# Convolution of the later batches in fp16 halves: three half-precision products in place of one fp32 product

## The chip, the cores and the metric

The kernel runs on one core of one Trainium2 chip. The metric is device time in microseconds, from three runs of a kernel. The engines are PE (TensorE, the matrix engine), DVE (VectorE), ACT (ScalarE), POOL (GpSimd) and SP (SyncE, which here only starts transfers). ACT and POOL start transfers too. Each engine works through its own list of instructions in order and waits on semaphores for the others.

## The reference

The input `x` is 8 batches of 4224 tokens of 192 numbers in fp32. The work for each batch is a short causal convolution over tokens (7 taps, one set of taps for each of 8 heads of 24 columns), then the real part of a two-dimensional Fourier transform added to its input, a normalisation, and a two-layer perceptron with a residual:

```
w = softmax(weight, axis=-1)                     # (8 heads, 7 taps)
x_pad = concat([zeros(B, 6, D), x], axis=1)
conv[b, s, h, g] = sum_k w[h, k] * x_pad[b, s + k, h, g]
mixed = real(fft(fft(conv, axis=1), axis=2))
u = conv + mixed
un = (u - mean(u)) / sqrt(var(u) + 1e-6)
out = u + maximum(un @ w_ch1, 0) @ w_ch2
```

## The kernel before

**The convolution.** `conv_unit` (L400) works on a chunk of six windows of 120 tokens. A chunk lies in SBUF as `xt`, 128 rows (120 tokens and the ones ahead of them) by six windows by 192 columns, in fp32. For a head, one fp32 product of the banded matrix `band[:, h, :120]` (128 rows by 120 columns) with the 144 columns of that head (6 windows of 24) gives the head's output in the PSUM tile `pc`; L419 is that product. Three heads share one `pc`, so a chunk has three parts (3, 3 and 2 heads), and ACT carries each part from PSUM to `xa` (L428). From there a transfer writes it to `sc` in device memory, from which the Fourier stage reads it in another order. There are six chunks in a batch. The last batch computes seven heads this way, and the eighth on DVE (`conv_segments`).

**Batches overlap.** The main loop goes through steps; there are nine for a batch, numbered by `it` (the last is a short one). A step runs the perceptron for 512 tokens: six `ph` groups of five products (L792), each carried out of PSUM by ACT as `hh` (L796) and by DVE as `hlo` (L797, the rounding error of `hh`), and the `po` products of the step before (L811, L814, L817), whose sums DVE adds to `u` (L823). Between these units the loop spreads the front work of later batches: the convolution (one chunk in a step, over six steps), the loads of `xs` and their split into fp16 halves `XH` (ACT, L530) and `XL` (DVE, L538), and the first Fourier stage `pa` (L555, out of PSUM as `yh` and `yl`). The second stage `pb` (L581, carried out as `V`), the third `pq` (L678, added to `u` by DVE), and the normalisation come further on: DVE takes the statistics `mv`, POOL makes `v`, `y`, `un` and `hl` of them (L723 to L749), and a transposing transfer on SP (L763) turns `hl` into `kt`, which the `ph` products read. Batches 0 and 1 go through a start of their own, ahead of the loop or in its first steps.

**What sets the order.** The builder places each instruction in its engine's list when it builds the program, by its own estimate of when the inputs are there; the code only says what comes ahead of what. So code that is added in one place can move instructions elsewhere. The PSUM tiles `pc`, `pa`, `pb`, `pq` and `pn` share four buffers (tag `f`), `ph` has two, and `po` two.

**Norms.** `squares` (L357) squares a chunk on ACT and leaves the sum of each row in `nrm`. At the end of a batch's convolution `pow2_of_norm` (L211) adds these over all rows with a product by a matrix of ones (L218, `pn`), and takes the power of two `s_x` from it, by which `XH` and `XL` are scaled.

Of the kernel before, what the change touches and what calls it, by code (L numbers as in the profile page):

```python
# [126 lines left out]
def kernel(  # L127
# [30 lines left out]


# [199 lines left out]
    def squares(bt, x, behind=None):  # L359
        if bt.nsq == 0:  # L360
            bt.nrm = sb.tile([128, NCH + 1], F32, tag="nrmx", name=f"nrm_{bt.b}")
        n = x.shape[1] if len(x.shape) == 2 else x.shape[1] * x.shape[2]
        sq = sb.tile(
            [128, 1152], mybir.dt.bfloat16, tag="sq", name=f"sq_{bt.b}_{bt.nsq}", bufs=1
        )[:, :n]
        if len(x.shape) == 3:
            sq = sq.rearrange("p (w d) -> p w d", w=x.shape[1])
# [30 lines left out]

    def conv_unit(bt, ch, part, xa_slot=("xa", 2), slot=("f", 4), home=None):

        b = bt.b
# [15 lines left out]
        with after(staged.get("pe") if b == 1 else None):  # L417
          for h in range(h0, h0 + n):
            nc.tensor.matmul(  # L419
                pc[:WR, h - h0], band[:, h, :WR], xt[:, :, h * GRP : (h + 1) * GRP],  # L420
                start=True, stop=True,
            )
# [686 lines left out]
```

## Time and profile before

| | |
|---|---|
| time, median of 3 runs | 1238.72 us (1238.15 to 1240.5) |
| the profiled execution's own time | 1238.39 us |
| its span, from the first to the last instruction | 1236.6 us |
| mean granted clock of PE | 0.983 |
| PE busy | 1171.4 us (95%) |
| DVE, POOL, ACT busy | 818.3 us (66%), 768.3 us (62%), 595.6 us (48%) |
| products of the convolution | 756 records, two for each fp32 product |

Busy time of PE is the time in which at least one product is under way. Products overlap in the pipeline, so the duration of one (286 ns for a record of the fp32 convolution) is longer than its share of PE's time; what counts there is the distance from one start to the next. Idle time is put down to what ended it.

### The profile page before, as it was taken

What the parts mean: (1) busy time and instruction counts of PE and PEld (TensorE: products, weight loads), DVE (VectorE), ACT (ScalarE), POOL (GpSimd) and SP (SyncE); (2) the same over time, 40 slices, a digit from 0 to 9 for tenths busy, and PEclk for the clock granted to TensorE, in tenths of its full rate; (3) what the DMA queues carried; (4) which work ended last, traced back from release to release, by engine and by line L of the source; (5) the groups of instructions that cost most, each with busy time, mean ns of one, the idle gap of its engine ahead of it and who ended that gap; (6) DMA issues with size and microseconds to landing.
All of it is one profiled execution on the core that took longest, in us unless ns stands there. A gap on an engine that the chain in (4) does not pass through costs nothing.

```text
span 1236.6 us, 30122 instructions
## 1 busy us (share of the span) xinstructions
PE 1171.4 (95%) x12236; PEld 928.6 (75%) x12236; DVE 818.3 (66%) x1871; ACT 595.6 (48%) x983; POOL 768.3 (62%) x1103
## 2 busy tenths in 40 slices
PE   5289869999999999999999999999999999999998
PEld 4178657787878777787787878787687877787776
DVE  6777655687656975478656876468965687567543
ACT  5675545365544555446543565445454455333222
POOL 0207676479637785468854796467963688667840
PEclk9599989999999999999999999999999999999999
DMA  8964985566455756377645675557754643323321
GB/s 297 271 189 115 240 125 114 128 173 185 93 123 149 186 140 140 87 181 188 144 96 138 157 194 100 123 144 185 150 99 100 164 99 90 83 63 81 81 56 42
DMA packets 238506, 170.47 MB, mean 138 GB/s; under 512 B 119512, under 2 KB 222112, under 8 KB 238368
## 3 DMA queue, kind: packets, MB, share of 16 engines
q1 hardware_dynamic: 184888, 109.95, 38.9%
q10 hardware_dynamic: 46952, 45.24, 13.4%
q0 software_dynamic: 6528, 13.38, 4.4%
q8 instruction: 95, 1.56, 0.5%
q14 instruction: 43, 0.35, 0.1%
HBM read 83.82 MB, written 58.55 MB: 115 GB/s over the span
## 4 chain that ended last, share of the span: by engine, by line
PE 85%; DVE 7%; DMA 4%; ACT 1%; issue 1%; POOL 1%; SPq 1%; DVEq 0%; ACTq 0%; POOLq 0%
PE ph L792 32%; PE po L811 10%; PE po L817 10%; PE po L814 10%; PE pa L555 6%; PE pb L581 6%; PE pq L678 6%; PE pc L419 6%; DVE XL L538 1%; DMA xs<-sc 1%; DVE yl L564 1%; DVE hlo L797 1%; DVE u L696 1%; DMA xs_yh<-sc 1%; ACT XH L530 1%
## 5 line engine op out<-in xcount | busy, mean ns | idle before, releaser
L792 PE MATMUL ph<-kt,W 128*128 128x512 f16 (+1 forms) x2160 | 494.9, 362 | 8.6 <-DVE hlo L797 7.0
L797 DVE SCALAR_TENSOR_TENSOR hlo<-ph,hh 128x512 f16<-128x512 f32 (+1 forms) x400 | 271.3, 679 | 279.0 <-ACT hh L796 271.1
L796 ACT ACTIVATE hh<-ph 128x512 f16<-128x512 f32 (+1 forms) x400 | 237.0, 593 | 432.1 <-PE ph L792 422.0
L811 PE MATMUL po<-W,hh 128*128 128x192 f16 x1584 | 386.1, 246 | 9.6 <-ACT hh L796 9.6
L814 PE MATMUL po<-W,hh 128*128 128x192 f16 x1584 | 385.6, 246 | 0.0
L817 PE MATMUL po<-W,hlo 128*128 128x192 f16 x1584 | 384.6, 246 | 0.0
L792 PEld LDWEIGHTS <-W 128*128 128x128 f16 x2160 | 192.7, 98 | 149.3 <-issue 9.1
L732 POOL TENSOR_SCALAR un<-u,mv,y 128x192 f32<-128x192 f32 x260 | 270.4, 1046 | 6.5 <-POOL y L728 0.2
L627 POOL DMA_INDIRECT u<-sc,rows_sb x136 | 145.6, 1071 | 68.1 <-DMA xs_yh<-sc 37.2
L811 PEld LDWEIGHTS <-hh 128*128 128x128 f16 x1584 | 155.4, 98 | 27.2 <-ACT hh L796 10.2
L817 PEld LDWEIGHTS <-hlo 128*128 128x128 f16 x1584 | 154.8, 98 | 22.3 <-issue 0.8
L814 PEld LDWEIGHTS <-hh 128*128 128x128 f16 x1584 | 155.0, 98 | 16.8
L723 POOL TENSOR_SCALAR v<-mv 128x4 f32<-128x4 f32 (+1 forms) x71 | 24.5, 344 | 176.9 <-DVE mv L704 147.3
L419 PE MATMUL pc<-xt,band 128*120 128x144 f32 x724 | 113.0, 295 | 13.4 <-DMA band<-line_d 11.0
L749 POOL TENSOR_TENSOR hl<-un,hl 128x512 f16<-128x512 f32 (+2 forms) x142 | 121.2, 874 | 4.0
L419 PEld LDWEIGHTS pc<-xt,band 128*120 128x120 f32 x724 | 99.9, 188 | 19.9 <-issue 10.9
L538 DVE SCALAR_TENSOR_TENSOR XL<-xs,s_x,XH 128x768 f16<-128x768 f32 (+1 forms) x56 | 94.7, 1692 | 29.3 <-ACT XH L530 29.3
L601 POOL COPY V<-V 128x96 f16<-128x96 f16 x64 | 16.8, 264 | 151.3 <-DVE V L592 151.2
L696 DVE SCALAR_TENSOR_TENSOR u<-pq,g,u 128x128 f32<-128x128 f32 (+1 forms) x328 | 102.7, 378 | 12.1 <-PE pq L678 12.1
L563 ACT ACTIVATE yh<-pa 99x512 f16<-99x512 f32 x128 | 75.9, 598 | 66.1 <-PE pa L555 61.8
L555 PE MATMUL pa<-c_sb,XH 128*128 128x128 f16 x1024 | 102.1, 220 | 0.9 <-ACT XH L530 0.9
L530 ACT ACTIVATE XH<-xs,s_x 128x768 f16<-128x768 f32 (+1 forms) x56 | 93.6, 1683 | 17.3 <-DMA xs<-sc 17.3
(135 smaller groups left out, 1551.1 us busy)
## 6 DMA issues: line engine op xcount, KB each, us to landing
out_dram<-u SPq DMA_DIRECT2D x64, 384.0 KB
xt<-in_xw_dram ACTq DMA_DIRECT2D x30, 576.0 KB
sc<-xa ACTq DMA_DIRECT2D x30, 540.0 KB
xs<-sc SPq DMA_DIRECT2D x28, 288.0 KB
u<-sc SPq DMA_DIRECT2D x72, 96.0 KB
xt<-in_xw_dram SPq DMA_DIRECT2D x10, 576.0 KB
sc<-xa SPq DMA_DIRECT2D x10, 540.0 KB
xs<-sc SPq DMA_DIRECT2D x28, 192.0 KB
```

The source lines that it names most:

```text
L419: nc.tensor.matmul(pc[:WR, h - h0], band[:, h, :WR], xt[:, :, h * GRP : (h + 1) * GRP], start=True, stop=True,)
L555: nc.tensor.matmul(pa[:, i], x[:, at], F[:, l], start=(n == 0), stop=(n == 2))
L627: nc.gpsimd.indirect_dma_start(to, None, bt.sc[:S], bass.IndirectOffsetOnAxis(ap=rows_sb[:, col : col + 1], axis=0),)
L696: nc.vector.scalar_tensor_tensor(to, src, bt.g, to, op0=ALU.mult, op1=ALU.add)
L732: (nc.vector if b + it == 0 else nc.gpsimd).tensor_scalar(un[:, g], u[:, g], mv[:, g, 0:1], y[:, g : g + 1], op0=ALU.subtract, op1=ALU.mult,)
L749: lower = (nc.vector if b + it == 0 else nc.gpsimd).tensor_tensor(bl[:, :, o : o + n], un[:, :ng, f], hi[:, :, f], op=ALU.subtract)
L792: nc.tensor.matmul(ph[:, n], W1[:, w, ht * 128 : (ht + 1) * 128], kt[:, k], start=(i == 0), stop=(i == len(order) - 1),)
L796: anchor[0] = nc.scalar.activation(hh, ph, AF.Relu).ins
L797: nc.vector.scalar_tensor_tensor(hlo, ph, 0.0, hh, op0=ALU.max, op1=ALU.subtract)
L811: nc.tensor.matmul(po[:, g % 2], hh[:, ht, tk], W2[:, ht, 0], start=(ht == 0), stop=False)
L814: nc.tensor.matmul(po[:, g % 2], hh[:, ht, tk], W2[:, ht, 1], start=False, stop=False)
L817: nc.tensor.matmul(po[:, g % 2], hlo[:, ht, tk], W2[:, ht, 0], start=False, stop=(ht == 5),)
```

## The change

From batch 2 on, a chunk is first split into two fp16 halves. `split_windows` squares `xt` as before, sums the squares over all rows with a product by ones (`pn`, L414 of the changed kernel), and makes a power of two `c` of the sum with integer operations on the bits (three small DVE operations `wr`, `wr`, `wc`; a fourth, `wg`, gives the factor that undoes it). ACT writes `xh`, the upper half of `c*xt`, and DVE writes `xl`, what is left of it, in two instructions. The band is split once, into `halves_of_band`, scaled by 2 to the 14. A head's convolution is then three fp16 products, with the upper band on `xh`, the upper band on `xl`, and the lower band on `xh`, added in PSUM; the band has 128 columns there instead of 120. ACT's way out of PSUM (`xa`) multiplies by `wg`. The product `xl` times the lower band is left out.

The split of a chunk is issued one step ahead of its convolution, and its `xt` is loaded one step earlier in turn. The squares of these batches no longer stand beside the convolution; they are the first part of the split. The ones and the sums of squares are bf16 in all norms, so a `pn` is one pass. Batches 0 and 1 keep the fp32 product.

```diff
+KB = 14
+RSQRT = float(0x5F3759DF + (15 << 23))
...
+    halves_of_band = cp.tile([128, 2, NH, WP], F16, name="halves_of_band")
...
+    def split_windows(bt, ch):
+
+        xt = bt.xt.pop(ch)
+        n = xt.shape[2]
+        xh = sb.tile([WP, WC, D], F16, tag="sq", name=f"xh_{bt.b}_{ch}", bufs=1)
+        xl = sb.tile([WP, WC, D], F16, tag="xl", name=f"xl_{bt.b}_{ch}", bufs=1)
+        i = bt.nsq
+        squares(bt, xt, sq=xh.bitcast(BF16)[:, :, :n])
+        tot = sb.tile([128, 1], BF16, tag="tot", name=f"tot_{bt.b}_{ch}")
+        nc.vector.tensor_scalar_max(tot, bt.nrm[:, i : i + 1], 1e-30)
+        pn = ps.tile([128, 512], F32, tag="f", name=f"pn_{bt.b}_{ch}", bufs=4)
+        nc.tensor.matmul(pn[:, :1], ones, tot, start=True, stop=True)
...
+        nc.vector.tensor_scalar(
+            ri, pn[:, :1].bitcast(I32), 1, None, op0=ALU.logical_shift_right
+        )
+        nc.vector.tensor_scalar(ri, ri, -1.0, RSQRT, op0=ALU.mult, op1=ALU.add)
+        nc.vector.tensor_scalar(
+            c.bitcast(I32), ri, 0x7F800000, None, op0=ALU.bitwise_and
+        )
+        nc.vector.tensor_scalar(
+            g.bitcast(I32), c.bitcast(I32), -1.0, float((254 - KB) << 23),
+            op0=ALU.mult, op1=ALU.add,
+        )
+        with in_turn():
+            nc.scalar.activation(xh[:, :, :n], xt, AF.Copy, scale=c)
+        for w in (slice(0, 3), slice(3, 6)):
+            nc.vector.scalar_tensor_tensor(
+                xl[:, w, :n], xt[:, w], c, xh[:, w, :n],
+                op0=ALU.mult, op1=ALU.subtract,
+            )
+        bt.xt[ch] = (xh[:, :, :n], xl[:, :, :n], g)
...
     def conv_unit(bt, ch, part, xa_slot=("xa", 2), slot=("f", 4), home=None):
...
           for h in range(h0, h0 + n):
+            g = slice(h * GRP, (h + 1) * GRP)
+            if b > 1:
+                for i, (w, x) in enumerate(((0, xt), (0, xl), (1, xt))):
+                    nc.tensor.matmul(
+                        pc[:, h - h0], halves_of_band[:, w, h], x[:, :, g],
+                        start=(i == 0), stop=(i == 2),
+                    )
+                continue
             nc.tensor.matmul(
-                pc[:WR, h - h0], band[:, h, :WR], xt[:, :, h * GRP : (h + 1) * GRP],
+                pc[:WR, h - h0], band[:, h, :WR], xt[:, :, g],
                 start=True, stop=True,
             )
...
-            if bt.b > 1 and ch + 2 < NCH:
-                units.append(call(load_windows, bt, ch + 2))
+            if bt.b > 1 and ch + 1 < NCH:
+                units.append(call(split_windows, bt, ch + 1))
+            if bt.b > 1 and ch + 3 < NCH:
+                units.append(call(load_windows, bt, ch + 3))
...
+            if rel == min(conv) - 1:
+                units.append(call(split_windows, bt, 0))
+                units.append(call(load_windows, bt, 2))
...
+    with after(leading["hi"]), after(leading["lo"]):
+        nc.scalar.activation(halves_of_band[:, 0], band, AF.Copy, scale=2.0 ** KB)
+        nc.vector.scalar_tensor_tensor(
+            halves_of_band[:, 1], band, 2.0 ** KB, halves_of_band[:, 0],
+            op0=ALU.mult, op1=ALU.subtract,
+        )
```

Three places of the engines' lists, each before and with the change. Names end in a running number that means nothing; `pc_3_4_0` is the part that begins with head 0, of chunk 4, of batch 3.

**PE, the first part of chunk 4 of batch 3.** Before, its three heads are one run of fp32 products behind the `po` of the perceptron:

```order
L817 MATMUL po_1_4_0_4761<-W2_364,hlo_1_4_4419 128x192
L419 MATMUL pc_3_4_0_4893<-xt_3_4_4416,band_103 120x144 x3
L792 LDWEIGHTS W1_316
```

With the change, the sum of squares stands ahead of the second Fourier stage of batch 2, and the products of the part come further on, each with a weight load:

```order
L848 MATMUL ph_1_5_1_5152<-kt_1_5_4531,W1_317 128x512
L414 LDWEIGHTS ones_66
L414 MATMUL pn_3_4_5064<-tot_3_4_5062,ones_66 128x1
L637 LDWEIGHTS yh_2_4378
...
L465 LDWEIGHTS halves_of_band_72
L465 MATMUL pc_3_4_0_5218<-xh_3_4_5059,halves_of_band_72 128x144
L848 LDWEIGHTS W1_317
...
L465 MATMUL pc_3_4_0_5218<-xl_3_4_5060,halves_of_band_72 128x144
```

In PE's list there are 34 `po` and 7 `ph` products from the end of `ph_1_4_5` (the last group ahead of the squares on ACT) to `pn_3_4`, and 36 `pq`, 27 `pb`, 18 `po` and 3 `ph` products from there to the first `pc_3_4_0`. The first product on `xh` stands apart from the rest of its part, with five `ph` and some `po` products between.

**ACT and DVE, the split of that chunk.** Before, ACT squares the chunk beside its convolution:

```order
L590 ACTIVATE V_2_0_4786<-pb_2_0_1_4805 128x102x4
L796 ACTIVATE hh_1_5_4746<-ph_1_5_1_4822 128x512
L369 ACTIVATE sq_3_4_4890,nrm_3_3802<-xt_3_4_4416 128x1152
L428 ACTIVATE xa_3_4_4892<-pc_3_4_0_4893 120x3x6x24
```

With the change ACT has the squares (L373), and three instructions later the upper half (L432), ahead of a `V` and two `hh`:

```order
L852 ACTIVATE hh_1_4_4719<-ph_1_4_5_5051 128x512
L373 ACTIVATE xh_3_4_5059,nrm_3_3811<-xt_3_4_4361 128x1152
L852 ACTIVATE hh_1_5_5076<-ph_1_5_0_5078 128x512
L646 ACTIVATE V_2_0_5114<-pb_2_0_0_5115 128x102x4
L432 ACTIVATE xh_3_4_5059<-xt_3_4_4361,wc_3_4_5067 128x1152
L646 ACTIVATE V_2_0_5114<-pb_2_0_1_5133 128x102x4
L852 ACTIVATE hh_1_5_5076<-ph_1_5_1_5152 128x512
```

and DVE has these, of which none was there before but the `hlo`, the `V` and the `u`:

```order
L412 TENSOR_SCALAR tot_3_4_5062<-nrm_3_3811 128x1
L853 SCALAR_TENSOR_TENSOR hlo_1_5_5077<-ph_1_5_0_5078,hh_1_5_5076 128x512
L420 TENSOR_SCALAR wr_3_4_5066<-pn_3_4_5064 128x1
L423 TENSOR_SCALAR wr_3_4_5066<-wr_3_4_5066 128x1
L424 TENSOR_SCALAR wc_3_4_5067<-wr_3_4_5066 128x1
L427 TENSOR_SCALAR wg_3_4_5068<-wc_3_4_5067 128x1
L648 SCALAR_TENSOR_TENSOR V_2_0_5114<-pb_2_0_0_5115,V_2_0_5114 128x102x4
L434 SCALAR_TENSOR_TENSOR xl_3_4_5060<-xt_3_4_4361,wc_3_4_5067,xh_3_4_5059 128x576 x2
L648 SCALAR_TENSOR_TENSOR V_2_0_5114<-pb_2_0_1_5133,V_2_0_5114 128x102x4
L752 SCALAR_TENSOR_TENSOR u_1_8_4433<-pq_1_8_5160,g_1_1283,u_1_8_4433 128x192
```

So the squares moved about a step ahead, and `xl` stands on DVE behind the copy `xh` on ACT.

**POOL, in the first steps of the loop (batch 0, steps 4 to 6).** Before, the reading of the statistics of step 6 (`v_0_6`) stands between two parts of `hl_0_4`:

```order
L732 TENSOR_SCALAR un_0_4_1573<-u_0_4_937,mv_0_4_1453,y_0_4_1546 128x192 x4
L746 CAST hl_0_4_1599<-un_0_4_1573 128x4x192
L723 TENSOR_SCALAR v_0_6_1982<-mv_0_6_1900 128x4
L749 TENSOR_TENSOR hl_0_4_1599<-un_0_4_1573,hl_0_4_1599 128x4x128
L749 TENSOR_TENSOR hl_0_4_1599<-un_0_4_1573,hl_0_4_1599 128x4x64
```

With the change it comes behind `un_0_5`:

```order
L788 TENSOR_SCALAR un_0_4_1626<-u_0_4_938,mv_0_4_1479,y_0_4_1599 128x192 x4
L802 CAST hl_0_4_1652<-un_0_4_1626 128x4x192
L805 TENSOR_TENSOR hl_0_4_1652<-un_0_4_1626,hl_0_4_1652 128x4x128
L805 TENSOR_TENSOR hl_0_4_1652<-un_0_4_1626,hl_0_4_1652 128x4x64
L788 TENSOR_SCALAR un_0_5_1884<-u_0_5_1182,mv_0_5_1734,y_0_5_1840 128x192 x4
L779 TENSOR_SCALAR v_0_6_2097<-mv_0_6_1996 128x4
```

On SP's list the transposition of `hl_0_4` stands ahead of the loads of the last two pieces of `xs` of batch 1, before and with the change. On DVE's list `mv_0_5` stood ahead of the first `XL` of batch 1 before, and stands behind it with the change; the load of chunk 3 of batch 2, which ACT started behind the third of these `XH`, is now started ahead of the first.

More of the change, by code (lines that the diff above doesn't have):

```diff
@@ L12 @@
 F32 = mybir.dt.float32
+BF16 = mybir.dt.bfloat16
 I32 = mybir.dt.int32
@@ L148 @@
     )
-    ones = cp.tile([128, 128], F32, name="ones")
+    ones = cp.tile([128, 128], BF16, name="ones")
     nc.vector.memset(ones, 1.0)
@@ L189 @@
     nc.vector.reciprocal(w8, w8)
-    line = sb.tile([NH, 2 * WP], F32, tag="pr", name="line", bufs=1)
+    line = sb.tile([NH, 2 * WP], F32, tag="un", name="line", bufs=1)
     nc.vector.memset(line, 0.0)
@@ L211, in pow2_of_norm @@
     def pow2_of_norm(parts, n, exponent, name):
-        tot = sb.tile([128, 1], F32, tag="nrm", name=f"tot_{name}", bufs=8)
-        nc.vector.tensor_reduce(tot, parts[:, :n], axis=AX.X, op=ALU.add)
+        tot = sb.tile([128, 1], BF16, tag="tot", name=f"tot_{name}")
+        with nc.allow_low_precision(reason="only the power of two next to it is used"):
+            nc.vector.tensor_reduce(tot, parts[:, :n], axis=AX.X, op=ALU.add)
         tag, bufs = ("h", 2) if name[0] == "w" else ("f", 4)
@@ L357, in load_windows, with squares @@
         bt.xt[ch] = xt
-    def squares(bt, x, behind=None):
+    def squares(bt, x, behind=None, sq=None):
         if bt.nsq == 0:
             bt.nrm = sb.tile([128, NCH + 1], F32, tag="nrmx", name=f"nrm_{bt.b}")
[L362 to L367, printed above, removed]
+        if sq is None:
+            sq = sb.tile(
+                [128, WC, D], BF16, tag="sq", name=f"sq_{bt.b}_{bt.nsq}", bufs=1
+            )[:, :, : x.shape[2]]
         with tc.issue_after(behind) if behind else in_turn():
@@ L397, in scratch @@
         bt.sc = dp.tile([S + DUP, D], F32, tag="sc", name=f"sc_{bt.b}", bufs=3)
+    def split_windows(bt, ch):
[9 more added lines that the diff above has]
+        nc.tensor.matmul(pn[:, :1], ones, tot, start=True, stop=True)
+        r, c, g = (
+            sb.tile([128, 1], F32, tag=f"w{k}", name=f"w{k}_{bt.b}_{ch}")
+            for k in "rcg"
+        )
+        ri = r.bitcast(I32)
+        nc.vector.tensor_scalar(
[17 more added lines that the diff above has]
+        bt.xt[ch] = (xh[:, :, :n], xl[:, :, :n], g)
     def conv_unit(bt, ch, part, xa_slot=("xa", 2), slot=("f", 4), home=None):
         b = bt.b
-        xt = bt.xt[ch]
+        xt, xl, back = bt.xt[ch] if b > 1 else (bt.xt[ch], None, 1.0)
+        if b > 1:
+            back = back[:WR]
         if part == 0:
@@ L405, in conv_unit @@
                 scratch(bt)
-            if b != 1:
-                squares(bt, xt, None if b or ch == 0 else bt.evicted)
+            if b == 0:
+                squares(bt, xt, bt.evicted if ch else None)
             bt.xa[ch] = home or sb.tile(
@@ L427, in conv_unit @@
             with after(leading.get("hi", staged.get("act")) if b == 1 else None):
-                bt.evicted = nc.scalar.activation(to, pc[:WR, :n], AF.Copy).ins
+                bt.evicted = nc.scalar.activation(
+                    to, pc[:WR, :n], AF.Copy, scale=back
+                ).ins
         if part == 2:
@@ L440, in conv_segments @@
         acc = sb.tile([128, SR, DH], F32, tag="xs", name=f"sg_{bt.b}", bufs=4)
-        squares(bt, x.rearrange("p r d -> p (r d)"))
+        squares(
+            bt, x.rearrange("p r d -> p (r d)"),
+            sq=acc.rearrange("p r d -> p (r d)").bitcast(BF16)[:, : SH * DH],
+        )
         for i in range(NH - HP):
```

6 lines of the change are left out of this document (4 added, 2 removed).

## The prediction

> **What bounds the kernel now.** I read the page's busy times first, then the stages, then PE's own waits, then the pace of PE's products, and last the one stretch where PE stands still.
>
> ```profile
> PE 1171.4 (95%) x12236; PEld 928.6 (75%) x12236; DVE 818.3 (66%) x1871; ACT 595.6 (48%) x983; POOL 768.3 (62%) x1103
> ```
>
> An average says little, so here are stages of the stretches view (columns: window, its length, busy time and instructions of PE, weight loads, DVE, ACT, POOL, granted clock, DMA share, GB/s): three whole batches, and the time in which batch 1 comes in.
>
> ```profile
> 250.00:390.00 140.00, 140.00 (x1490) 112.15 (x1487) 95.56 (x218) 72.57 (x120) 93.05 (x133) 1.00 0.57 143
> 390.00:530.00 140.00, 140.00 (x1492) 112.03 (x1490) 93.29 (x202) 72.51 (x119) 96.42 (x138) 1.00 0.58 140
> 530.00:670.00 140.00, 140.00 (x1473) 111.67 (x1471) 94.92 (x216) 71.66 (x117) 94.70 (x136) 1.00 0.59 142
> ...
> 140.00:160.00 20.00, 16.31 (x138) 11.93 (x138) 16.49 (x29) 14.82 (x20) 11.69 (x13) 1.00 0.66 168
> 160.00:180.00 20.00, 10.61 (x90) 7.59 (x89) 6.62 (x8) 6.97 (x9) 17.21 (x21) 0.74 1.10 173
> ```
>
> In the whole batches PE has a product under way all the time, at full clock, while DVE, ACT and POOL rest a third to a half of theirs. From 140 to 180 us it is otherwise: 13 us idle, and a low clock. All waits of PE from 110 us to the end (who, for whom, total, times, longest):
>
> ```profile
> PE po L811 <- ACT hh L796: 9.6, 3, 8.7
> PE ph L792 <- DVE hlo L797: 7.0, 6, 3.1
> PE ph L792 <- DMA kt<-hl: 1.7, 1, 1.7
> PE pa L555 <- ACT XH L530: 0.7, 1, 0.7
> PE pa L555 <- DVE XL L538: 0.3, 1, 0.3
> ```
>
> That is 19.3 us in all, 8.7 of it in one piece. So from 180 us on the time is the sum of PE's products, each at its pace, and a product taken away is time gained, as long as the work that is added elsewhere doesn't make PE wait.
>
> **The change, part by part.**
>
> *Products.* The pace is the distance between starts. Timeline rows of PE (start, length, line, count), with a run of conv records and a run of `po` (the first and the last of 17):
>
> ```profile
> 421.07 1.17 PE L419 MATMUL pc<-xt,band 128*120 128x144 f32 x8
> 422.07 0.56 PE L678 MATMUL pq<-c_sb,V 128*128 128x130 f16 x7
> ...
> 423.63 0.25 PE L811 MATMUL po<-W,hh 128*128 128x192 f16 x1
> ...
> 424.95 0.25 PE L814 MATMUL po<-W,hh 128*128 128x192 f16 x1
> ```
>
> Eight records take 422.07 - 421.07 = 1.00 us, and a head is two: 250 ns. A `po` of 192 columns takes 1.32/16 = 82.5 ns with its weight load. The chain of waits gives the pace at 128 columns, and the length of a batch, from the same piece of `pa` in two batches:
>
> ```profile
> 455.11 1.35 PE pa L555 x24
> 599.69 1.36 PE pa L555 x24
> ```
>
> 1.35/24 = 56 ns, and 144.6 us a batch. On the line through 56 (128 columns) and 82.5 (192) a product of 144 columns takes 63 ns, so a head takes 189 ns, 61 less. Heads concerned: batches 2 to 6 have 6 chunks of 8, batch 7 has 6 of 7, in all 282. Gain 282 x 61 ns = 17.2 us. Bounds: no cheaper than 128 columns (168 a head, 23.1 us), no dearer than 192 (247.5 a head, 0.7 us). I take the line, as 144 lies near 128.
>
> *Sums over rows.* 36 times a `pn` is added on PE. The row of before is the fp32 one, in two records:
>
> ```profile
> 969.10 0.28 PE L218 MATMUL pn_x<-tot_x,ones 128*128 128x1 f32 x2
> 969.24 0.24 PE L811 MATMUL po<-W,hh 128*128 128x192 f16 x1
> ```
>
> 0.14 us for two, 0.07 for the one pass of bf16: 36 x 0.07 = 2.5 us (at the price of two 5.0, at nothing 0). Sum on PE: 17.2 - 2.5 = 14.7 us less.
>
> *ACT and DVE.* Nearest rows (busy, mean ns of one):
>
> ```profile
> L369 ACT ACTIVATE sq<-xt 128x1152 bf16<-128x1152 f32 (+1 forms) x46 | 52.7, 1145 | 2.8 <-DMA xt<-in_xw_dram 2.8
> L369 ACT ACTIVATION_READ_ACCUMULATOR sq<-xt 128x1 f32 x46 | 9.1, 198 | 0.0
> L336 DVE SCALAR_TENSOR_TENSOR W<-w,s_w,W 128x576 f16<-128x576 f32 x2 | 1.5, 816 | 0.5 <-ACT W L335 0.5
> L255 DVE SCALAR_TENSOR_TENSOR w<-cv_w,cv_w 128x576 f32<-128x576 uint32 x2 | 1.5, 745 | 0.0
> L538 DVE SCALAR_TENSOR_TENSOR XL<-xs,s_x,XH 128x768 f16<-128x768 f32 (+1 forms) x56 | 94.7, 1692 | 29.3 <-ACT XH L530 29.3
> L224 DVE TENSOR_SCALAR s_x<-r_x 128x1 int32<-128x1 int32 x8 | 1.2, 151 | 0.2
> ```
>
> ACT gains a copy of the size of the squares, 1.15 us a split, 41 us in all, against some 68 of 140 us idle per batch. DVE gains two `xl` of 576 elements at 0.82 (same operation and size in L336; 0.75 from L255, 1.27 by elements from L538) and five small ones at 0.15: 2.4 us a split (2.2 to 3.3), 86 us in all, from 66 to 73%. What hides this is the idle time of both under PE. It is thinnest on DVE in the three steps where `XL` is made, which are also steps with a split:
>
> ```profile
> 402.90:418.70 15.80, 15.80 (x188) 12.25 (x186) 15.36 (x40) 9.36 (x14) 9.58 (x17) 1.00 0.72 166
> 418.70:434.60 15.90, 15.90 (x140) 12.23 (x139) 13.27 (x29) 9.44 (x14) 15.32 (x22) 1.00 0.71 193
> 434.60:451.00 16.40, 16.40 (x154) 12.24 (x152) 11.05 (x19) 10.32 (x16) 15.02 (x18) 1.00 0.76 188
> ```
>
> 15.36 + 2.4 is 2.0 more than the first step's 15.8; the second just holds its own (15.7 of 15.9); the third takes the 2.0 back (13.5 of 16.4). So DVE can run 2 us late for about two steps of each batch, and what is late next is `hlo`, which frees the two `ph` buffers and feeds `po`. PE loses between nothing (DVE was 97% busy in that step before and PE did not wait) and 2.0 us a batch, 0 to 12 us over six batches. I take 3, near the low end, because `hlo` has a spare `ph` buffer and the order puts it between the small operations.
>
> *The waits in the split.* Five `ph` in the chain of waits:
>
> ```profile
> 409.88 1.08 PE ph L792 x5
> ```
>
> and `hh` in the groups:
>
> ```profile
> L796 ACT ACTIVATE hh<-ph 128x512 f16<-128x512 f32 (+1 forms) x400 | 237.0, 593 | 432.1 <-PE ph L792 422.0
> ```
>
> For chunk 4 of batch 3 PE has, from the last `ph` ahead of the squares to `pn`, 34 `po` (2.8 us) and 7 `ph` (1.5 us): 4.3 us. The chain there is `hh`, squares, read-out, `tot`: 0.60 + 1.15 + 0.20 + 0.15 = 2.1 us. From `pn` to the chunk's first product PE has 18 `po` (1.5), 3 `ph` (0.65), 27 `pb` of 102 columns and 36 `pq` of 65 (by columns, against the 56 ns of 128: 1.2 and 1.0), in all 4.4 us, against three small operations, the copy and both `xl`: 0.45 + 1.15 + 1.64 = 3.2 us. Behind a waiting `pn` stand `pb` and `pq`, and behind the copy on ACT a `V` and two `hh`; with 2.2 and 1.2 us to spare I price these waits at nothing, and what they cost when ACT or DVE is late is in the 0 to 12. The band's halves (1024 elements once on ACT and on DVE, 1.0 to 2.3 us by the time for an element in the rows of L369 and L538) fall before 110 us, and go into the same 3.
>
> *The start.* The long wait of PE has a chain in the timeline: `hl_0_4` on POOL, its transposition on SP, the loads of `xs` behind that, then `XH` on ACT.
>
> ```profile
> 154.32 1.41 POOL L723 TENSOR_SCALAR v<-mv 128x4 f32<-128x4 f32 x1 [8.05 <-DVE mv L704]
> 155.81 2.94 POOL L749 TENSOR_TENSOR hl<-un,hl 128x512 f16<-128x512 f32 x2
> 158.78 3.66 SPq L763 DMA_TRANSPOSE kt<-hl  x1
> 162.53 2.94 SPq L489 DMA_DIRECT2D xs<-sc  x4
> 169.12 1.59 ACT L530 ACTIVATE XH<-xs,s_x 128x768 f16<-128x768 f32 x1 [10.35 <-DMA xs<-sc]
> 170.62 0.57 ACT L796 ACTIVATE hh<-ph 128x512 f16<-128x512 f32 x1
> ```
>
> POOL waits 8.05 us for statistics of step 6 with `hl_0_4` half done, and by the new order that wait stands behind `hl_0_4`. What `hl_0_4` waits for then is `mv_0_5`, now behind the first `XL`, which ends at about 140 us, and 9 to 10 us of POOL's own work: it ends near 150 instead of 158.75, so `XH` finds its rows some 8 us sooner. Against that, a load of 576 KB (chunk 3 of batch 2) now comes ahead of these `xs`, 3.4 us at the 173 GB/s of that stretch. PE wins back 4.6 us of the 8.7, and part of what it loses at the low clock behind it (10.6 busy us at 0.74, up to 2.8): I take 7. Bounds: 11.5 if all of it goes, and 3.4 lost if only the load counts.
>
> *Sum*, against the profiled execution's own 1238.39 us (span 1236.6 and 1.8 around it; the median of the runs is 0.3 higher): 1238.4 - 14.7 - 7 + 3 = 1219.7. I say 1219.
>
> A rule that speaks against this: the Trainium skill, page "TensorE: Matmul & The Clock Gate", section "Back-to-back issue gap", has streams of weight load and product at about 81 ns for 128 columns and 131 for 512. By it a product of 144 columns is an estimated 83 ns, a head 249, and the gain on PE nothing: the sum would be near 1237. This case's `pa`, which are such pairs, show 56 ns.
>
> **The rivals.**
>
> *The stretch at 140 to 180 us stays as it is*, with another engine late in its place. For it: DMA is at 1.10 there, and ACT and DVE get the splits of chunks 1 to 3 in the same stretch. Against it: the row that held POOL has moved. 1238.4 - 14.7 + 3 = 1227, and 1230 if the load ahead of `xs` costs its 3.4.
>
> *DVE stands still for the copy.* On DVE `xl` is next but one behind `wg`; if DVE has nothing to do until ACT's copy is there, a split costs it 2.4 + 1.15 = 3.6 us, and the three full steps overflow by 3.4 and 1.0 before the third recovers: 4.4 a batch, 26 in six. 1238.4 - 14.7 - 7 + 26 = 1243, slower than before. It decides from 3.6 us a batch on (21.7/6). For it: 97% in the first step. Against it: a `V` or `hlo` is placed in that gap, and PE waited there for nothing before.
>
> *Weight loads set the pace.*
>
> ```profile
> L814 PEld LDWEIGHTS <-hh 128*128 128x128 f16 x1584 | 155.0, 98 | 16.8
> ```
>
> If a product could start only every 98 ns, a head would take 294, 44 more than now: 12.4 us lost, 1238.4 + 12.4 + 2.5 - 7 + 3 = 1249. Against it: `pa` and `po` have the same loads and run at 56 and 82.5. The rule of the skill above is its milder form.
>
> *The change doesn't do what it says* I leave out: PE's new list has the 846 fp16 products.
>
> **How the numbers follow.** What a measurement of this kernel can tell from no change is about 0.2%, 2.5 us. Forecast 0.67 (1219, own range 1211 to 1226), the start unchanged 0.20, DVE 0.09, weight loads 0.04. Faster by over 0.2% is the first two, 0.87; of DVE's case half lies within 0.2%: same 0.05, slower 0.08. Range: 1209 (line at its cheap side and most of the start's 11.5) to 1232 (start unchanged with the load's price, and 2 us of waits); it leaves out DVE's bad half, the weight loads and the ends of the forecast.
>
> **What would show it.** The chain's rows of `pa` a batch apart should be 144.6 - 48 x 0.061 + 6 x 0.07 = 142.1 us apart; a distance of 144 or more says that the products or the waits went wrong. Runs of the new products should start every 63 ns (56: better; 83: the skill's rule; 98: weight loads). PE's own waits past 180 us should stay under 8 us in all; DVE's `hlo` as their cause is the second rival. The 8.05 us on POOL should be gone, ACT's wait for `xs` should fall from 10.35 to about 2 or 3, and the granted clock from 160 to 180 us should rise above 0.74. The prediction falls if the pace is above 80 ns, or if a split costs PE more than 0.6 us (21.7/36).

## The result, and the profile after

| | before | with the change |
|---|---|---|
| time, median | 1238.9 us (1238.15 to 1240.5, 4 runs) | 1230.5 us (1229.2 to 1233.6, 4 runs) |
| the profiled execution's own time, and its span | 1238.39 us, 1236.6 us | 1233.64 us, 1231.9 us |
| ratio of the times | | 0.9938, 95% interval 0.9917 to 0.9959 |

Ratios are taken over runs in the chip's usual, faster state alone, so they need not equal the quotient of the medians.

The change gains 8.4 us. The forecast of 1219 us meant 19.9 from the same median. The direction was right, and the time is inside the range, near its upper end. The busy times, first row of the page of the changed kernel:

```profile
PE 1154.5 (94%) x12544; PEld 910.3 (74%) x12544; DVE 882.8 (72%) x2124; ACT 644.3 (52%) x1020; POOL 800.3 (65%) x1103
```

PE's busy time fell by 1171.4 - 1154.5 = 16.9 us, a little more than the 14.7 of the forecast. The span fell by 4.7 only, so PE's idle time grew by 12.2 us. The same stretches as before show where (window, length, busy time and instructions of PE, weight loads, DVE, ACT, POOL, granted clock, DMA share, GB/s):

```profile
140.00:160.00 20.00, 15.18 (x132) 11.17 (x131) 12.64 (x28) 12.92 (x15) 17.69 (x22) 0.91 1.06 209
160.00:180.00 20.00, 17.37 (x168) 12.46 (x166) 16.23 (x29) 13.46 (x20) 14.84 (x16) 1.00 0.60 168
250.00:390.00 140.00, 136.23 (x1500) 106.78 (x1498) 103.72 (x254) 77.74 (x123) 98.32 (x136) 1.00 0.67 145
390.00:530.00 140.00, 136.26 (x1525) 107.94 (x1523) 105.49 (x258) 79.95 (x124) 98.74 (x131) 1.00 0.64 142
530.00:670.00 140.00, 136.28 (x1531) 108.00 (x1530) 103.13 (x244) 80.57 (x124) 100.34 (x135) 1.00 0.63 137
```

From 140 to 180 us PE is busy 5.6 us longer than before, and the granted clock is 0.91 and 1.00 where it was 1.00 and 0.74. But in every stretch of 140 us, where PE had no pause at all before, it now pauses for 3.7 us. PE's waits from 180 us to the end (who, for whom, total, times, longest):

```profile
PE ph L848 <- DVE hlo L853: 12.2, 11, 1.5
PE pc L465 <- DVE xl L434: 6.5, 5, 1.9
PE po L867 <- DVE u L879: 1.7, 5, 0.4
PE pc L465 <- ACT xh L432: 0.4, 1, 0.4
```

Those are 20.8 us. The same view of the kernel before has 4.4:

```profile
PE ph L792 <- DVE hlo L797: 4.1, 3, 3.1
PE pa L555 <- DVE XL L538: 0.3, 1, 0.3
```

So the account of the 4.7 us is: 16.9 less work, 16.4 more waiting past 180 us, and (65.2 - 4.4) - (77.4 - 20.8) = 4.2 less idle time ahead of that. A batch takes as long as ACT's rows of the same `hh` are apart (start, length, engine, line, and the idle time before with its cause):

```profile
398.94 0.60 ACT L852 ACTIVATE hh<-ph 128x512 f16<-128x512 f32 x1 [2.27 <-PE ph L848]
544.67 0.60 ACT L852 ACTIVATE hh<-ph 128x512 f16<-128x512 f32 x1 [2.27 <-PE ph L848]
```

145.7 us, 1.1 more than before, though its products should take 2.9 less. A mean says nothing yet of the place. Steps are numbered 0 to 8 here, as `it` is. In step 0 of batch 2 DVE's timeline has these rows (x3 is three instructions in one row), and PE's the two below them:

```profile
404.94 1.55 DVE L752 SCALAR_TENSOR_TENSOR u<-pq,g,u 128x192 f32<-128x192 f32 x5
406.40 1.85 DVE L594 SCALAR_TENSOR_TENSOR XL<-xs,s_x,XH 128x768 f16<-128x768 f32 x1
408.15 0.86 DVE L759 BATCH_NORM_STATS2 st<-u 128x6 f32<-128x192 f32 x3
408.92 0.68 DVE L853 SCALAR_TENSOR_TENSOR hlo<-ph,hh 128x512 f16<-128x512 f32 x1
409.77 1.55 DVE L594 SCALAR_TENSOR_TENSOR XL<-xs,s_x,XH 128x768 f16<-128x768 f32 x1
...
409.66 1.24 PE L848 MATMUL ph<-kt,W 128*128 128x512 f16 x5 [1.49 <-DVE hlo L853]
412.15 1.24 PE L848 MATMUL ph<-kt,W 128*128 128x512 f16 x5 [0.76 <-DVE hlo L853]
...
415.20 0.16 DVE L412 TENSOR_SCALAR tot<-nrm 128x1 bf16<-128x1 f32 x1 [0.45 <-issue]
```

An `XL` stands between `u` and `hlo`, so 4.0 us pass on DVE from the first `u` until that `hlo` starts, and PE waits for the `ph` buffer. The last row is the first operation of a split on DVE in this step; the one before it came in step 6 of batch 1. It stands behind both waits of PE, so it was not the split's own work or waits on DVE that made that `hlo` late, but what stands ahead of it in DVE's list. In the same step of the kernel before, both `XL` came later, behind an `hlo` each:

```profile
412.26 0.67 DVE L797 SCALAR_TENSOR_TENSOR hlo<-ph,hh 128x512 f16<-128x512 f32 x1
...
413.27 1.84 DVE L538 SCALAR_TENSOR_TENSOR XL<-xs,s_x,XH 128x768 f16<-128x768 f32 x1
...
416.74 0.67 DVE L797 SCALAR_TENSOR_TENSOR hlo<-ph,hh 128x512 f16<-128x512 f32 x1
...
418.80 1.54 DVE L538 SCALAR_TENSOR_TENSOR XL<-xs,s_x,XH 128x768 f16<-128x768 f32 x1
```

### The profile page after: what moved, and what is told of

Read it like the earlier page. It is cut to its first block, busy times and chain, and to the rows that moved or that the text cites. A ratio compares the mean times of both kernels' runs of the same rounds, so it can differ in the third digit from the quotient of the medians.

```text
span 1231.9 us, 31047 instructions
## 1 busy us (share of the span) xinstructions
PE 1154.5 (94%) x12544; PEld 910.3 (74%) x12544; DVE 882.8 (72%) x2124; ACT 644.3 (52%) x1020; POOL 800.3 (65%) x1103
## 4 chain that ended last, share of the span: by engine, by line
PE 72%; DVE 13%; DMA 6%; ACT 4%; issue 4%; SPq 1%; ACTq 0%; DVEq 0%
PE ph L848 28%; PE po L867 8%; PE po L873 8%; PE po L870 8%; PE pa L611 6%; PE pb L637 5%; PE pq L734 5%; PE pc L465 3%; DVE XL L594 3%; DMA sc<-xa 3%; DVE u L752 2%; DVE hlo L853 1%; DVE st L759 1%; ACT XH L586 1%; DVE xl L434 1%
## 5 line engine op out<-in xcount | busy, mean ns | idle before, releaser
L848 PE MATMUL ph<-kt,W 128*128 128x512 f16 (+1 forms) x2160 | 494.0, 361 | 16.9 <-DVE hlo L853 12.9
L867 PE MATMUL po<-W,hh 128*128 128x192 f16 x1584 | 381.9, 246 | 3.1 <-DVE u L879 2.9
L870 PE MATMUL po<-W,hh 128*128 128x192 f16 x1584 | 381.9, 246 | 0.0
L848 PEld LDWEIGHTS <-W 128*128 128x128 f16 x2160 | 191.7, 98 | 155.3 <-issue 14.9
L788 POOL TENSOR_SCALAR un<-u,mv,y 128x192 f32<-128x192 f32 x260 | 285.1, 1102 | 7.5 <-POOL y L784 0.2
L683 POOL DMA_INDIRECT u<-sc,rows_sb x136 | 155.2, 1141 | 68.4 <-DMA xs_yh<-sc 36.8
L657 POOL COPY V<-V 128x96 f16<-128x96 f16 x64 | 20.1, 318 | 147.4 <-DVE V L648 147.3
L779 POOL TENSOR_SCALAR v<-mv 128x4 f32<-128x4 f32 (+1 forms) x71 | 18.1, 255 | 138.8 <-DVE mv L760 130.6
L594 DVE SCALAR_TENSOR_TENSOR XL<-xs,s_x,XH 128x768 f16<-128x768 f32 (+1 forms) x56 | 91.7, 1638 | 14.8 <-ACT XH L586 14.8
L611 PE MATMUL pa<-c_sb,XH 128*128 128x128 f16 x1024 | 99.1, 220 | 0.1
L734 PE MATMUL pq<-c_sb,V 128*128 128x130 f16 (+1 forms) x1440 | 96.5, 216 | 1.6 <-ACT V L646 1.6
L879 DVE SCALAR_TENSOR_TENSOR u<-po,fo,u 128x384 f32<-128x384 f32 (+1 forms) x136 | 80.8, 594 | 23.5 <-PE po L873 23.4
```

The costliest lines, as they stand in the source:

```text
L594: nc.vector.scalar_tensor_tensor(part(XL), src, bt.c, part(XH), op0=ALU.mult, op1=ALU.subtract)
L611: nc.tensor.matmul(pa[:, i], x[:, at], F[:, l], start=(n == 0), stop=(n == 2))
L683: nc.gpsimd.indirect_dma_start(to, None, bt.sc[:S], bass.IndirectOffsetOnAxis(ap=rows_sb[:, col : col + 1], axis=0),)
L734: mm = nc.tensor.matmul(po, weights(v, ND * r + k3), rhs[:, 0] if it == Q0 else rhs, start=(r + n == 0), stop=(r == 1 and n == 2),)
L788: (nc.vector if b + it == 0 else nc.gpsimd).tensor_scalar(un[:, g], u[:, g], mv[:, g, 0:1], y[:, g : g + 1], op0=ALU.subtract, op1=ALU.mult,)
L848: nc.tensor.matmul(ph[:, n], W1[:, w, ht * 128 : (ht + 1) * 128], kt[:, k], start=(i == 0), stop=(i == len(order) - 1),)
```

## The experiments

Since the start of the program differs from kernel to kernel by up to 20 us, each run is read by two numbers: its time, and the distance between batches (the `hh` that begins step 0, batch 1 to batch 5, median of four; 144.6 us before, 145.6 with the change). Ratios are to the kernel before on the same chip.

| kernel | time, us | ratio (95%) | a batch, us |
|---|---|---|---|
| the change | 1230.5 | 0.994 (0.992 to 0.996) | 145.6 |
| no_xl | 1227.1 | 0.990 (0.988 to 0.991) | 144.2 |
| const_scale | 1224.7 | 0.988 (0.986 to 0.989) | 143.3 |
| shift | 1274.7 | 1.029 (1.025 to 1.033) | 150.1 |
| prod_only | 1239.2 | 0.998 (0.996 to 1.000) | 143.3 |
| prod_half_xl | 1258.5 | 1.010 (1.005 to 1.016) | 149.7 |
| const_small | 1226.5 | 0.990 (0.988 to 0.992) | 143.2 |
| gap | 1215.1 | 0.981 (0.979 to 0.984) | 142.4 |
| before_pool | 1229.8 | 0.993 (0.991 to 0.994) | 144.6 |
| pn_unread | 1235.7 | 0.998 (0.996 to 0.999) | 145.2 |
| one_unit | 1234.7 | 0.997 (0.995 to 0.999) | 145.9 |
| gap_chain | 1214.9 | 0.980 (0.978 to 0.982) | 142.6 |
| merged | 1242.5 | 1.002 (1.000 to 1.003) | 146.9 |
| prod_merged | 1218.1 | 0.980 (0.977 to 0.983) | 142.1 (141.3 where no pause falls) |
| before_unit | 1242.6 | 1.001 (1.000 to 1.003) | 144.3 |
| before_first | 1233.6 | 0.996 (0.994 to 0.997) | 146.4 |

### Work of DVE, or its waits in the chain?

The first two theories were that DVE has too much to do in the steps with `XL` (A), or that it stands in the split's chain (B). Three kernels take parts of the split away, and shift moves the convolution to other steps. In no_xl the loop with the two `xl` is deleted and `xl = xh`; the others are these edits of the changed kernel:

```diff
 # const_scale: from tot to wg, all left out
+        c, g = 1.0, 2.0 ** -KB
 # prod_only: as const_scale, and without the copy and xl
-        bt.xt[ch] = (xh[:, :, :n], xl[:, :, :n], g)
+        bt.xt[ch] = (xh[:, :, :n], xh[:, :, :n], g)
 # shift
-    conv_at = {r: [r + 17] for r in range(-17, -11)}
+    conv_at = {-15: [0], -14: [1, 2], -13: [3, 4], -12: [5]}
```

> The changed kernel without the two `xl` instructions of each split; the second product of each head takes `xh` once more, so PE's work is the same and the lower halves of the rows are left out of the result. Theory A (DVE's added work makes `hlo` late in the three steps with `XL`, some 3.5 us a batch): 1.64 of the 2.4 us that a split adds to DVE are gone, so nearly all of that goes, 1230.5 - 6 x 3.3 = about 1211 us, and the distance of a batch falls from 145.6 to about 142.5 us. Theory B (not the work, but DVE's waits in the chain for `pn` and for the copy): the waits for `pn` stay, about half the loss stays, 1221 us and 144 us a batch. Theory C (the start and the order of the lists, not the splits): 1230 us and 145.6 us a batch.

> The changed kernel with the constants 1 and 2 to the -14 in place of the power of two of each chunk: `tot`, `pn`, `wr`, `wr`, `wc` and `wg` are left out of each split (so the scale no longer follows the rows), the squares, the copy and both `xl` stay. Theory A (work of DVE): 0.75 of 2.4 us are gone, a third of the loss goes, 1230.5 - 6 x 1.2 - 1 for the 36 `pn` = about 1222 us, 144.3 us a batch. Theory B (waits in the chain): the wait for `pn` is gone and the copy no longer stands behind it, 1211 us, 142.5 us a batch. Theory C: 1229 us.

> The changed kernel with another table for the convolution: its six chunks in four steps (1, 2, 2, 1 chunks from the third step on) instead of six, so that the splits fall into steps 2 to 5 of the nine instead of 0 to 5, and one instead of three of them into steps with `XL`. Theory A (DVE's work in the steps with `XL`): most of the 3.5 us a batch goes, 1230.5 - 15 = 1215 us. Theory B (waits in the chain): two splits follow each other in one step with one `xh` and one `xl` buffer, so the chain is waited for more often, 1230 to 1240 us. Theory C: no change but for the start, 1225 to 1235 us.

> The products alone: the changed kernel without the split's chain, copy and `xl`. PE does the same 846 fp16 products, on whatever the buffer of the squares holds, so the result of the convolution is left out; the squares and the loads stay. Theories A and B: all of the loss goes, batches are 141.6 to 142 us apart, and the time is 1230.5 - 20 - 1 = 1207 to 1212 us. Theory C, or a price of the products that was taken wrongly: batches 144 us apart or more and 1220 us or more.

Neither theory met its numbers in all three: no_xl met B's 144 us a batch but not its time, and const_scale fell between the two. The greater work went with no_xl, and it brought 1.4 us a batch; the small operations and `pn` brought 2.3. That speaks against A. But the products alone, where A and B both said 141.6 to 142, came 143.3 us apart, and one batch of that kernel has this for PE (its waits, one batch from 558.67 us):

```profile
PE ph L821 <- DVE u L725: 1.4, 1, 1.4
PE ph L821 <- DVE hlo L826: 0.2, 1, 0.2
```

So 1.6 us a batch are waited for with no split at all on DVE. (One of the four batches has a pause of 3.8 us besides and takes 149.8.) The time of 1239 us comes from one wait of 15.1 us for a `kt` near 140 us, in the start. Shift fell in another way: with two chunks in a step `kt` comes late all along (PE's waits, whole run), which is no verdict on A or B.

```profile
PE ph L848 <- DMA kt<-hl: 28.7, 13, 3.7
```

The next four: prod_half_xl writes `XL` for half the columns, const_small puts five small operations without any wait into const_scale, gap spreads the chain over the step with the convolution first in it, before_pool changes only the start.

```diff
 # const_small, beside the constants
+        for k in range(5):
+            nc.vector.tensor_scalar_max(<128x1>, minus_half[:, 0:1], 1e-30)
 # gap: the units of a step, in this order
+  conv_unit x3; squares, tot, pn | one unit | wr, wr, wc, wg | half the rest | copy, xl; load | the rest
 # before_pool
+            with after(lows.get(4) if b * NIT + it == 6 else None):
                 P.tensor_scalar(v, var, LNEPS, None, op0=ALU.add)
```

> The products alone, as in the run before, and from batch 2 on `XL` is written for half of its columns only, so that DVE has 8 x 0.85 = 6.8 us less to do a batch in the steps with `XL` (the result is then wrong in that part too). The products alone came 143.15 us a batch where the sum of the products says 141.65. Theory D (once PE is faster, DVE's own work in the three steps with `XL` sets the pace there, so half of what the products give is not collected): 141.7 us a batch. If the products were priced too low instead: 143.1 us a batch, as before.

> The kernel with constant scales, and in each split five small DVE operations on a constant, which wait for nothing and whose results nobody reads: DVE has the same work as in the changed kernel, without `tot`, `pn` and the wait for it. Constant scales gave 143.4 us a batch (three batches: 144.7, 143.2, 143.5) and 1224.7 us. Theory B (it is the wait for `pn` in DVE's list, not the work): 143.4 to 143.7 us a batch, 1225 to 1227 us. Theory A (the work): 145.0 us a batch and 1230 us or more.

> The changed kernel with the same instructions in another order: the convolution of a step comes first among the units that are spread over the step, behind it the squares, `tot` and `pn` of the next chunk, a unit later `wr`, `wr`, `wc` and `wg`, and in the middle of the step the copy and `xl`. So more of other work lies between the links of the chain. Theory B (waits for `pn` and for the copy): 143.5 to 144.3 us a batch and 1218 to 1225 us. Theory A (DVE's work): 145.5 us a batch, 1230 us. The start can add some us to either by its own order.

> The kernel before with one edit: POOL takes up `v` of the seventh group (v_0_6) only behind the last operation of `hl_0_4`. If that wait of 8.05 us on POOL is what holds the start, as the prediction has it, 8 to 12 us go (the changed kernel had gained 12.4 us on the kernel before between the steps 2 and 5): 1227 to 1231 us, and the batches stay 144.6 us apart. If another engine takes its place: 1237 to 1240 us.

Prod_half_xl is inconclusive: its lists came out in another order, and it waits for `kt` (5 times in the whole run, 34.3 us), which the products alone do only once, in the start. Const_small is against A: with all of DVE's added work but no wait for `pn`, a batch takes 143.2 us, the same as the products alone in the same order of units. Its waits of PE between 250 and 830 us, four batches, are 6.6 us against 14.9 with the change:

```profile
PE ph L834 <- DVE hlo L839: 5.2, 7, 1.4
PE ph L834 <- DVE u L738: 1.4, 1, 1.4
```

Gap has all of the change's instructions and takes 142.4 us a batch, 1215.1 us. That is even less than B said (143.5 to 144.3 us and 1218 to 1225), and it changed two things: the room in the chain, and the place of the convolution. Before_pool gains 9.2 us by its ratio and leaves the batches at 144.6, as expected of the start.

### Room between `pn` and `wr`, or the place in the step?

```diff
 # pn_unread
-            ri, pn[:, :1].bitcast(I32), 1, None, op0=ALU.logical_shift_right
+            ri, usual.bitcast(I32), 1, None, op0=ALU.logical_shift_right
 # one_unit: between pn and the first wr one unit of the perceptron, otherwise as the change
 # gap_chain: the units of a step, in this order
+  conv_unit x3 | half the rest | squares, tot, pn, wr, wr, wc, wg, copy, xl; load | the rest
```

> The changed kernel with one operand changed: the first `wr` of each split reads a constant (128 x 1152, a usual sum of squares) in place of `pn`. All instructions stay, `tot` and `pn` among them, but DVE no longer waits for PE there (so the scale no longer follows the rows). Theory B (the wait for `pn` in DVE's list): 143.2 to 143.7 us a batch, as with five small operations that wait for nothing, and 1222 to 1227 us. If it is the wait of DVE for the squares (`tot`) or of PE for `tot`: 144.5 us or more. Theory A (the work): 145.5 us.

> The changed kernel with one move: between `pn` and the first `wr` of a split stands one more unit of the perceptron's part of the step (the sums are one unit, scales, copy and `xl` the next). Theory B: part of the 13.3 us that DVE waited for `pn` between 250 and 830 us goes, and 143.5 to 144.8 us a batch come out, 1221 to 1227 us. Theory A: 145.5 us a batch, 1230 us.

> One of the two moves of the kernel that took 142.4 us a batch: the convolution first in its step, but the whole chain of the split in one piece in the middle of the step, `wr` directly behind `pn`. If the room between `pn` and `wr` made that gain: 144.5 to 145.5 us a batch, 1224 to 1232 us. If it was the place of the convolution and of the split in the step: 142.4 to 143 us a batch, 1214 to 1219 us.

Here B fell as the cause of the late `hlo`. Without the wait for `pn` the batches are 145.2 us apart, and PE still has the same waits for `hlo`, eight in four batches, 9.0 us as with the change (pn_unread, 250 to 830 us):

```profile
PE ph L850 <- DVE hlo L855: 9.0, 8, 1.5
PE ph L850 <- DMA kt<-hl: 2.2, 2, 1.6
PE po L869 <- issue: 1.5, 1, 1.5
```

The wait for `xl`, 4.6 us in these four batches with the change, is gone, so by this one edit that part does hang on `pn`; the 3.7 us for `kt` and without a cause came in its place. One more unit of room changed nothing for the better (145.9). Gap_chain, with the chain in one piece, takes 142.6 us a batch: what counted in gap was the place of convolution and split in the step. In one batch of gap_chain PE waits 0.8 us (392.82 to 535.39 us):

```profile
PE ph L858 <- DVE hlo L863: 0.6, 2, 0.4
PE po L877 <- ACT hh L862: 0.2, 1, 0.2
```

And DVE still stands for the copy there, for more than with the change (3.9), only not where PE needs it (DVE's waits, 250 to 830 us):

```profile
DVE xl L444 <- ACT xh L442: 11.2, 16, 1.2
```

### What moved `XL` ahead of `hlo`

The loop hands out its units by their number: `for f in fill[k * i // n : k * (i + 1) // n]` runs in `spread`, with `k` units over the `n` pieces of the step's main list, the perceptron's among them. In step 0 the change has two units more, the split of chunk 0 and the load of chunk 2, behind the `XL` units in the list; so each `XL` comes a piece earlier. That is theory E, and three kernels test it. Merged and prod_merged put load and split into one unit, so that steps 0 to 4 have as many units as before (step 5 has one more); before_unit adds empty ones to the kernel before.

```diff
 # merged, prod_merged: steps 1 to 5; in step 0 the load of chunk 1, the split of chunk 0, the load of chunk 2
+    def split_and_load(bt, ch):
+        split_windows(bt, ch)
+        if ch + 2 < NCH:
+            load_windows(bt, ch + 2)
 # before_unit: one in steps 1 to 5, two in step 0
+                units.append(lambda: None)
```

> The changed kernel with the same calls in as many units a step as the kernel before has: the load of a chunk is one unit with the split ahead of it (in the first step of a batch the load of chunk 1, the split of chunk 0 and the load of chunk 2 are one). In DVE's list the two `XL` pieces of the first step then stand behind `hlo` again, as in the kernel before. Theory E (two more units in the first step pull both `XL` pieces ahead of `hlo`): PE's 2.25 us a batch for `hlo` there go, 143.2 to 143.6 us a batch, 1215 to 1221 us; what stays is the wait for `xl`, 1.2 us a batch. Theory A or B (work or chain on DVE): 145.5 us a batch, 1230 us.

> The products alone, with as many units a step as the kernel before has (the result of the convolution is left out, as in the run of the products alone). Theory E: the 1.5 us a batch that were missing there come back, 141.6 to 141.9 us a batch. If they are missing because the products were priced too low or DVE is too full: 143.1 us a batch. The start is not judged by this run.

> The kernel before with empty units added to the list that is spread over a step: two in the first step of a batch, one in each of the next five. No instruction is added; in DVE's list the two `XL` pieces of the first step move ahead of `hlo`. Theory E: the first step loses what the products alone lost there, 1.7 us, so 146.2 us a batch and 1245 to 1252 us. Theories A and B: 144.6 us a batch, 1239 us.

With the products alone E holds: two batches in a row are 141.3 us apart, PE waits for nothing in them, and 144.58 - 141.34 = 3.2 us are collected. (The other two batches have a pause each, of 4.8 and 1.4 us, for which the trace shows no cause; behind the longer one the granted clock is lower, 0.94 from 300 to 330 us.) With the whole split it doesn't hold as expected. In merged the wait for `hlo` fell from 2.3 us a batch to 1.0, and the wait for `xl` rose from 1.2 to 2.6, as the split is now in the last unit of its step, nearer to its convolution in the next (PE, one batch from 546.48 us):

```profile
PE pc L465 <- DVE xl L434: 2.6, 2, 1.8
PE ph L848 <- DVE hlo L853: 1.0, 1, 1.0
PE po L867 <- DVE wg L427: 0.5, 1, 0.5
```

Before_unit was expected to lose 1.7 us a batch and lost nothing. DVE's list has the `XL` ahead of `hlo` there too, and PE has no wait in it. A likely reason is in PE's groups of that step (552.63 to 570.80 us): fp32 convolution stands there, and in the same step of prod_only there is none.

```profile
L419 PE MATMUL pc<-xt,band 128*120 128x144 f32 x16 | 2.5, 290 | 0.0
```

PE's own list of step 0 differs in a second way. In the change, and in no_xl, pn_unread, one_unit and merged, 24 `pb` (16 on `yh`, 8 on `yl`) and 18 `pq` products have moved out of that step. These are the groups of `pb` on `yh` and of `pq` in step 0 of batch 2, first of prod_only (408.86 to 426.4 us), then of the change (398.94 to 415.1 us):

```profile
L610 PE MATMUL pb<-c_sb,yh 99*128 99x102 f16 x48 | 4.0, 208 | 0.0
L707 PE MATMUL pq<-c_sb,V 128*128 128x130 f16 x36 | 2.4, 219 | 0.0
...
L637 PE MATMUL pb<-c_sb,yh 99*128 99x102 f16 x32 | 2.4, 208 | 0.0
L734 PE MATMUL pq<-c_sb,V 128*128 128x130 f16 x18 | 1.2, 219 | 0.0
```

The two differences together fit PE's waits in step 0: none with neither of them (prod_merged), 1.6 us with the early `XL` alone (prod_only, const_small), 1.0 with the moved products alone (merged), 2.3 with both (the change, no_xl, pn_unread). So E is one part of the loss. What moves the products was not tested; DVE's wait for `pn` does not, since pn_unread has them moved too. That the early `XL` costs only where PE has no other products to put beside it is read from these lists, and no edit tests it alone. The last question was whether the place of the convolution is a gain by itself; before_first is before_pool with the convolution first in its step:

```diff
+        fill = ahead + fill        # ahead: the conv_units of batch 2 and later
```

> The kernel before with two edits: POOL takes up v_0_6 only behind `hl_0_4` (that alone ran in 1229.8 us), and from batch 2 on the convolution stands first in its step. If PE's sum sets the pace there, the place of the convolution gives nothing with fp32 products: 144.3 to 144.6 us a batch, 1227 to 1232 us, and the 15 us down to 1214.9 us belong to the products, which the changed kernel had not collected. If the order is a gain of its own: 143 us a batch or less and 1222 us or less.

It is not: 1233.6 us, 3.9 more than before_pool, 146.4 us a batch. PE now waits for the rows, whose load follows too late (all waits past 100 us):

```profile
PE pc L419 <- DMA xt<-in_xw_dram: 6.7, 4, 2.5
PE pc L419 <- DMA xt<-in_xv_dram: 3.5, 1, 3.5
```

That is a new wait, so it leaves open whether fp32 products could use the place with an earlier load; in this form they lose. Gap_chain is, with gap, the best kernel of all, 24 us below the one before and 15.6 below the change, with the change's instructions and another order of units.

## Where the prediction was right, and where it failed

**Products: right.** A run of products (first row and last):

```profile
280.64 0.29 PE L465 MATMUL pc<-xh,halves_of_band 128*128 128x144 f16 x2
...
281.82 0.23 PE L465 MATMUL pc<-xh,halves_of_band 128*128 128x144 f16 x1
```

There are 19 steps from start to start in these 1.18 us: 62 ns, forecast 63. Prod_merged collects 3.2 us a batch where 48 x 61 ns = 2.9 were forecast. The rule of the Trainium skill, page "TensorE: Matmul & The Clock Gate", section "Back-to-back issue gap", by which a pair of 144 columns would take an estimated 83 ns, does not hold for these rows; nor does the rival by which weight loads set the pace.

**Sums over rows: too dear.** A `pn` holds PE up for 0.03 us in 29 of 36 places and for 0.07 to 0.10 in the others, 1.5 us in all and not 2.5:

```profile
271.93 0.17 PE L414 MATMUL pn<-tot,ones 128*128 128x1 bf16 x1
271.96 0.25 PE L637 MATMUL pb<-c_sb,yh 99*128 99x102 f16 x2
```

**ACT and DVE: the prices right, the sum wrong.** The groups have what was forecast: 0.82 for `xl`, 0.15 for a small operation, and 1.25 for the copy where 1.15 stood.

```profile
L434 DVE SCALAR_TENSOR_TENSOR xl<-xt,wc,xh 128x576 f16<-128x576 f32 x60 | 46.6, 817 | 8.2 <-ACT xh L432 5.2 <-issue 3.1
L432 ACT ACTIVATE xh<-xt,wc 128x1152 f16<-128x1152 f32 x30 | 37.5, 1249 | 8.9 <-DVE wc L424 8.1 <-issue 0.7
L420 DVE TENSOR_SCALAR wr<-pn 128x1 int32<-128x1 int32 x36 | 5.6, 157 | 21.3 <-PE pn L414 19.0 <-PE ph L848 1.6 <-issue 0.7
```

**This is the step that failed:** "PE loses between nothing (...) and 2.0 us a batch, 0 to 12 us over six batches. I take 3, near the low end, because `hlo` has a spare `ph` buffer and the order puts it between the small operations." One batch of the change (PE's waits, 398.94 to 544.67 us) has 3.8 us:

```profile
PE ph L848 <- DVE hlo L853: 2.3, 2, 1.5
PE pc L465 <- DVE xl L434: 1.2, 1, 1.2
PE po L867 <- DVE u L879: 0.3, 1, 0.3
```

Past 180 us it is 20.8 in all, 16.4 more than before the change and beyond the upper bound of 12. That is the miss: of the 13.9 us between the forecast of 1219.7 and the profiled execution's 1233.6, these waits make 16.4 - 3 = 13.4. The bound was made of DVE's work against the length of a step. Const_small shows that this work costs nothing measurable beside the products alone (143.2 against 143.3 us a batch), so the sum of busy times answered the wrong question. `hlo` was indeed what came late, but through the order of the lists in step 0 (the early `XL` on DVE, and on PE the products that had moved away), and the sentence on the order was taken from chunk 4 of batch 3, a step without `XL`. The new order was there to be read; the three steps that the term was about were read in the list of before.

**The waits in the split: failed too, by 1.2 us a batch.** They were priced at nothing with 1.2 us to spare, again at chunk 4. In step 1 chunk 0's split and its convolution are closer, and `pc` waits 1.2 us for `xl` there. In merged they are closer still, and `pc` waits in steps 1 and 2, 2.6 us together.

**The start: the size right, the parts not.** Seven were forecast. Before_pool, which has only the order on POOL, gains 9.2 us by itself, so the wait of 8.05 us was what held the start. With the change POOL's row is a wait of 4.33 us ahead of `hl_0_4`, which ends at 151.8 us instead of 158.75:

```profile
141.69 0.23 POOL L779 TENSOR_SCALAR v<-mv 128x4 f32<-128x4 f32 x1 [4.33 <-DVE mv L760]
...
150.07 1.77 POOL L805 TENSOR_TENSOR hl<-un,hl 128x512 f16<-128x512 f32 x2
...
150.97 1.63 ACT L586 ACTIVATE XH<-xs,s_x 128x768 f16<-128x768 f32 x1 [5.82 <-DMA xs<-sc]
```

ACT's longest wait for `xs` in that stretch is 5.8 us, not the 2 or 3 of the forecast. The first `hh` comes 4.0 us later than before, and by step 5 PE is 8.4 us ahead.

**What would show it** worked: a distance of 144 us or more was to say that the products or the waits went wrong, and waits past 180 us were to stay under 8. They are 20.8, the pace is right, so it was the waits.

**The rivals.** *DVE stands still for the copy* had nearly the size: 4.4 us a batch as it stands (its first overflow is 15.36 + 3.6 - 15.8 = 3.2 and not 3.4, which makes it 4.1), against 3.8 in the batch shown. But its mechanism is not this one, since gap_chain waits for the copy three times as long and PE waits 0.8 us a batch. It needed 21.7 us in all to make the change slower; the waits past 180 us grew by 16.4, as 4.4 us of the kernel before are gone from them. *The start stays* came near the time, 1227 to 1230 us, for a wrong reason.

**What stays open.** How much of the 3.8 us each move in the list is worth, since every edit moves several, and what moves the `pb` and `pq` products. Why merged doesn't keep the wait for `xl` as it was is read from its trace, not tested alone. The rest of gap_chain, 142.56 - 141.34 = 1.2 us a batch, is 0.8 of waits and 0.2 for six `pn`; the other 0.2 were not looked into.

## What to carry to other kernels

When a kernel hands out work by the number of units, a new unit moves its neighbours, and what must be read before pricing is the new list of each engine at the tightest place, not the busy time of that place. When the engine that sets the pace gets faster, orders that were hidden beside its work begin to cost; so try the place of the new work in the step before judging the change. Compare such kernels by the distance between repeated stages, because the start can move by more than the change is worth.

## What the runs showed beside that

A product of one column against the ones takes PE mostly 0.03 us between its neighbours, though the record shown is 0.17 us long. PE's gap of 1.49 us, which comes again in the same step of each batch, is a `ph` that finds both its buffers taken. By the Trainium skill, page "Perfetto Trace Analysis", section "Identifying Performance Opportunities", the same gap again and again can mean too few buffers. In gap_chain the longest such gap is 0.4 us with the same two buffers, so here it was when DVE freed them. And the start is touchy: the `hh` that begins step 2 of batch 0 comes at 128.2 us in the kernel before and at 150.6 with the products alone, so that the products alone, 1.3 us a batch faster than before, ended at the time of the kernel before.
